# Key and query tiles woven into the last value tiles, in a gated attention and token-mixing kernel

## The chip, the cores and the metric

The kernel runs on one core of one Trainium2 chip. The metric is the device time of one launch in microseconds (us), the median of several runs. A profile of one execution shows five engines: PE (TensorE, with its weight loads as PEld), DVE (VectorE), ACT (ScalarE), POOL (GpSimd) and SP (SyncE), which here issues all DMAs.

## The reference

The result is a gated sum of two branches over the same x of 2048 rows and 512 columns:

```python
g = sigmoid((x * gate_w).sum(-1, keepdims=True))
a = softmax_attention(x @ wqkv, 32 heads of 16) @ wo
b = (W2 gelu(W1 layernorm(x)^T))^T          # mixes the 2048 tokens, F = 1792
out = g * a + (1 - g) * b
```

Everything is float32. Branch a takes q, k and v from one product with wqkv, and the softmax runs over all 2048 keys for each head. Branch b's layer norm needs mean and variance of each row.

## The kernel before, in words

Each float32 operand of a product is split into a high and a low part, and three products (high-high, high-low, low-high) are added in PSUM. One product tile of 128x512 over the 512 columns is therefore 12 matmuls.

The order of work is written out by hand: each engine runs its instructions in the order in which the program states them, and an instruction that waits holds up all behind it on that engine. This is true of SP as well, so a DMA that waits for data or for a free buffer holds up the later DMAs.

First stage, the tiles of v. x comes in 16 tiles of 128 rows. Tiles 0 to 3 are turned on PE. For the others x is loaded a second time in blocks of 32x128 (`load_blocks`, L198), turned by DVE (`turn_blocks`, L203), cast to the high part on ACT and reduced to the low part on POOL (`split`, L83 and L84). Each tile of x also has its row statistics and its gate sum made on DVE (`row_stats`, L211 to L214). PE forms v for tile t (`products`, L91), and ACT copies it out of PSUM (`v_out`, L237). In this stage PE has seven rotating banks of PSUM (`bank`). In the loop over t from 2 to 15 each pass states, in this order: turn blocks of tile t+2, row statistics of t-2, load blocks t+5, load x t+3, and the product for t. At t = 5 it also sets six stripes of the three key buffers to -1 on POOL (L321); these are the rows that multiply the shift of each query in the scores. v is stored to DRAM in three pieces (L234).

Second stage, key and query tiles. There are 32 tiles T of 128 columns by 512 tokens: four for the keys of 8 heads, four for their queries, and so on, four tiles for each set j = T // 4 of weight columns. Each set of columns is loaded (`load_wcols`, L150) and split; two sets are split in the first stage, the next ones by `bring_wcols` with two cuts on DVE (L915, L919). `tile_alone` runs one tile: 12 matmuls (L939), a copy to SBUF on ACT (L941, two buffers `qraw`), a cast to the high part (L596), the low part by subtraction on DVE (L599), the greatest magnitude on DVE (L587), for queries an absolute value times the keys' greatest (L603), and a store of the parts (L611, four buffers `pc`). Tiles T = 0 to 9 run so, one behind the other. Then the first keys (`load_k`) and queries (`load_q`), stored to DRAM, are read back in stacked form, 6 and 8 DMAs each (L646). `copy_v` copies the first two pairs of v on POOL.

Third stage, attention with products beside. The scores (L730) use 64 rows of the array; the other 64 work on one half of a key or query tile, or later of the second layer (L744). A phase has 12 units of scores, ACT and DVE empty them (L713, L720, L709: DVE parks some in SBUF, ACT takes exponentials), and the weighted sum with v follows (L780, 48 matmuls for a phase of 12 units). The seven banks of the phases are planned at build time by a search (`plan_banks`, `State`), which runs a small model of PE, ACT and DVE and picks a bank for each unit. A first short phase of 8 units has no product beside it. Tile T = 10 is run whole within the second phase, by a hook ahead of its seventh unit, and the planner's model has a term for it. Tiles 11 to 31 run as products beside the scores, one in each two phases; their later steps are jobs that run on DVE at the end of phases with room.

After the first 8 of 16 groups of attention come the layer norm and the first product of branch b, then the other 8 groups beside the second product and the output projection.

Of the kernel before, what the change touches and what calls it, by code (L numbers as in the profile page):

```python
# [76 lines left out]
def gated_mix(ctx: ExitStack, tc: tile.TileContext, a_x, a_wqkv, a_wo, b_w1, b_b1, b_w2, b_b2, gate_w, out):  # L77
# [78 lines left out]

    qk_cols = [c0 + b * P for b in range(ND) for c0 in (D, 0)]
    qk_w = []
    x_load = None

    with tc.tile_pool(name="vp", bufs=1, side="right") as pool:
# [8 lines left out]
        wv = []  # L170

        def load_wv(k):
            raw = pool.tile([P, D], F32, name=f"wv_raw{k}")
            nc.sync.dma_start(raw, a_wqkv.rearrange("(p k) c -> p k c", k=ND)[:, k, 2 * D : 3 * D])
            wv.append((raw, pool.tile([P, D], F32R, name=f"wv_hi{k}"), pool.tile([P, D], F32R, name=f"wv_lo{k}")))
# [63 lines left out]
        with tc.manual_schedule():  # L239
# [9 lines left out]
            warm(6)  # L249
            load(0)  # L250
# [53 lines left out]
            for t in range(2, NS):  # L304
                if t + 1 < TURNED:
                    turn(t + 1)
                if t + 2 < NS:
                    turn_blocks(t + 2)
                row_stats(t - 2)
                if t + 5 < NS:  # L310
                    load_blocks(t + 5)
                if t + 3 < NS:
                    load(t + 3)
                if t == 4:
                    turn_biases(bias_tiles)
                if t == 5:
                    pool.tile([P, 40], F32, name="pad")
                    for ks in k_bufs:
                        for i in range(2):
                            at = i * HALF + SHIFT[0]  # L320
                            nc.gpsimd.memset(ks[at : at + DH].bitcast(F32), -1.0)  # L321
                if t in (6, 9):
                    qk_w.append(load_wcols(qk_cols.pop(0)))
                if t in (9, 12):
                    qk_w.append(split_wcols(*qk_w.pop(0)))
                if t in (NS - 3, NS - 1):
                    store_v(*((0, 8) if t == NS - 3 else (8, 13)))
# [3 lines left out]
            for t in range(NS - 2, NS):  # L331
                row_stats(t)
            store_v(13, NS)
# [33 lines left out]
    ALONE_PE, ALONE_ACT = 2.75, 1.9  # L367
# [10 lines left out]
    class State:  # L378
# [8 lines left out]
        def clear(self):  # L387
            self.kept, self.banks, self.avail, self.homes, self.done, self.alone, self.next = {}, (), {}, {}, {}, (), 0
# [51 lines left out]
        def score(self, n, ops, parked, u, bank, since, alone):  # L440
# [4 lines left out]
            for _ in range(alone):  # L445
                at = min(range(RING), key=lambda b: new.free[b])
                new.pe = max(new.pe + TURN, new.free[at]) + ALONE_PE + TURN
                new.act = max(new.act, new.pe) + ALONE_ACT
                new.free[at] = new.act
                new.alone += ((u, at),)  # L450
# [13 lines left out]
        def place(self, n, ops, parked, u, alone):  # L464

            if u in self.kept:
                bank, since = self.kept[u]
                return self.score(n, ops, parked, u, bank, since, alone)
            op = next(op for op in ops if u in op)
            out = []  # L470
            for bank in range(RING):
                if self.free[bank] < NEVER:
                    if len(op) == 2 and u not in parked:
                        for other in (bank - 1, bank + 1):
                            if 0 <= other < RING and self.free[other] < NEVER:
# [3 lines left out]
                                out += new.score(n, ops, parked, u, bank, new.free[bank], alone)  # L479
                    else:  # L480
                        out += self.score(n, ops, parked, u, bank, self.free[bank], alone)
# [35 lines left out]
        def close(self, blocks):  # L517
# [8 lines left out]
            self.log = self.log, ("s", self.banks, homes, pairs, self.alone)  # L526
# [7 lines left out]
    def plan_banks(phases, free):  # L534
# [3 lines left out]
        for n, blocks, sets_now, beside, alone in phases:  # L538
            ops, parked = PLANS[n]
            for u in range(n):  # L540
                found = {}
                for new in sorted((new for old in best for new in old.place(n, ops, parked, u, alone.get(u, 0))), key=State.worth):
# [19 lines left out]
    kmax, qmax = {}, {}  # L562

    def qk_tile(T):

        j, n = divmod(T, NQ)
        b, is_q = divmod(j, 2)
        return j, b, is_q, n

    def qk_pairs(T):  # L570
        j, b, is_q, n = qk_tile(T)
        cols = slice(n * NB, (n + 1) * NB)
        hi, lo = qk_w[j]
        for k in range(ND):
            w, x = (hi[:, k, :], lo[:, k, :]), (xt_hi[:, k, cols], xt_lo[:, k, cols])
            yield from ((w[0], x[0]), (w[0], x[1]), (w[1], x[0]))

    def qk_parts(T, raw, pc, alone):

        j, b, is_q, n = qk_tile(T)  # L580
        low, high = (2, 0) if is_q else (1, 0)
        if n == 0:
            (qmax if is_q else kmax)[b] = small.tile([P, NQ], F32, name="qmax" if is_q else "kmax")
        most_of = (qmax if is_q else kmax)[b]

        def greatest():
            nc.vector.tensor_reduce(most_of[:, n : n + 1], raw, axis=AX.X, op=ALU.max, apply_absolute_value=True)  # L587
            if n == NQ - 1:
                nc.vector.tensor_reduce(most_of[:, 0:1], most_of, axis=AX.X, op=ALU.max)
                if is_q:  # L590
                    nc.vector.tensor_mul(most[:, b : b + 1], most_of[:, 0:1], kmax[b][:, 0:1])
                else:
# [334 lines left out]
    with tc.manual_schedule(engines=engines):  # L927
# [20 lines left out]
        for T in range(BEFORE):  # L948
# [19 lines left out]
            if T == NQ + 1:  # L968
                load_q(0)
# [551 lines left out]
```

## Time and profile before

| what | value |
|---|---|
| median of 3 runs | 1269.43 us (1267.03 to 1271.43) |
| the profiled execution | 1270.11 us, of which the profile's span is 1267.3 us |
| mean granted TensorE clock | 0.991 |
| busy: PE, ACT, DVE, POOL | 1243.3, 1080.7, 776.9, 213.9 us |
| last copy of v out of PSUM | begins at 56.75 us |
| last matmul of tile T = 9 | begins at 83.52 us |
| first exponential of the scores | begins at 93.02 us |

Times in the profile count from the start of the span. A row of a timeline gives start, duration, engine, line, operation, result and operands, and in brackets how long the engine was idle before it and what released it. PE's durations overlap from one matmul to the next, so steps are read from start to start.

### The profile page before, as it was taken

To read this page: it belongs to the slowest core of one execution; us is meant where nothing else is said; L and a number is where in the kernel's file an instruction comes from. 1 tells how busy PE (TensorE), PEld (TensorE's weight loads), DVE (VectorE), ACT (ScalarE), POOL (GpSimd) and SP (SyncE) were. 2 spreads that over 40 slices of the span, in tenths; PEclk is the share of its full clock that TensorE was granted. 3 is DMA by queue.
4 is the path that set the end of the run, shared out by engine and by line. 5 is a ranking of instruction groups with operands and counts; after the bars stand their busy time and mean duration, and the time that the engine had idled before them with its cause. 6 is when DMAs were issued, how large, how long until landed. Compare 5 with 4: busy or idle time off the path is not lost.

```text
span 1267.3 us, 33265 instructions
## 1 busy us (share of the span) xinstructions
PE 1243.3 (98%) x13446; PEld 799.5 (63%) x13446; DVE 776.9 (61%) x1317; ACT 1080.7 (85%) x1562; POOL 213.9 (17%) x345
## 2 busy tenths in 40 slices
PE   9979999999999999999999999999999999999998
PEld 6755565666678887566655666566655666565656
DVE  6746887878885347455554555545545656557974
ACT  4358999999834336999999999999999999999990
POOL 4500000000045445011111111111111111100000
PEclk9989999999999999899999999999999999999999
DMA  6664443553364433143224433433433443526742
GB/s 200 242 205 135 118 125 109 136 144 90 132 214 131 128 105 102 28 110 98 75 69 119 98 83 76 103 73 94 105 83 92 112 128 89 108 70 175 173 143 87
DMA packets 169919, 149.17 MB, mean 118 GB/s; under 512 B 82055, under 2 KB 127261, under 8 KB 169502
## 3 DMA queue, kind: packets, MB, share of 16 engines
q1 hardware_dynamic: 169758, 146.97, 42.6%
q8 instruction: 108, 1.77, 0.6%
q14 instruction: 53, 0.43, 0.1%
HBM read 108.50 MB, written 38.39 MB: 116 GB/s over the span
## 4 chain that ended last, share of the span: by engine, by line
PE 93%; DMA 2%; DVE 2%; ACT 1%; SPq 1%; POOL 1%; issue 0%; ACTq 0%; DVEq 0%; POOLq 0%
PE s L780 36%; PE s L730 35%; PE s L1178 12%; PE dn L744 5%; PE s L939 2%; PE acc L91 2%; PE pa L1397 2%; DMA row<-bp 1%; ACT pt L713 1%; DMA gw<-in_gate_w_dram 1%; DMA qp<-pc 0%; POOL ks L321 0%; DVE quad L720 0%; SPq L198 0%; PE dn L1397 0%
## 5 line engine op out<-in xcount | busy, mean ns | idle before, releaser
L713 ACT ACTIVATE pt<-s 128x512 f32<-128x512 f32 (+1 forms) x1217 | 717.0, 701 | 4.2 <-PE s L730 1.7
L730 PE MATMUL s<-qs,ks 64*128 64x512 f32 x2048 | 527.8, 405 | 13.1 <-DMA qs<-qp 6.2
L730 PEld LDWEIGHTS s<-qs,ks 64*128 64x128 f32 x2048 | 353.8, 185 | 174.1 <-ACT pt L713 74.5
L720 DVE COPY quad<-s 128x512 f32<-128x512 f32 x616 | 400.8, 687 | 59.4 <-PE dn L744 33.5
L780 PE MATMUL s<-pt,vt 128*17 128x256 f32 x5728 | 423.3, 381 | 1.3 <-DVE quad L720 1.3
L709 ACT ACTIVATE quad<-quad 128x2048 f32<-128x2048 f32 x154 | 300.1, 1949 | 1.6 <-DVE quad L720 1.6
L780 PEld LDWEIGHTS s<-pt,vt 128*17 128x17 f32 x5728 | 181.5, 97 | 166.4 <-ACT pt L713 53.0
L792 DVE TENSOR_TENSOR ot<-s,ot 128x256 f32<-128x256 f32 (+1 forms) x155 | 79.4, 512 | 306.3 <-PE s L780 215.7
L744 PE MATMUL dn<-u,w_hi 64*128 64x512 f32 x768 | 255.9, 406 | 0.0
L780 PE MATMUL s<-quad,vt 128*17 128x256 f32 x2464 | 226.8, 379 | 0.0
L1009 POOL TENSOR_TENSOR w_lo<-w_raw,w_hi 128x512 fp32r<-128x512 f32 (+1 forms) x127 | 149.6, 1184 | 101.8 <-ACT w_hi L1006 78.4
L749 POOL MEMSET token<- 1x1 f32 x154 | 17.9, 116 | 870.5 <-PE dn L744 771.6
L744 PE MATMUL dn<-u,w_lo 64*128 64x512 f32 x384 | 155.9, 406 | 0.0
L780 PEld LDWEIGHTS s<-quad,vt 128*17 128x17 f32 x2464 | 100.9, 98 | 60.7 <-issue 0.8
L744 PEld LDWEIGHTS dn<-u,w_hi 64*128 64x128 f32 x768 | 136.3, 185 | 1.6 <-POOL token L749 0.2
L1178 PE MATMUL s<-h,w_hi 128*128 128x512 f32 x392 | 121.1, 390 | 0.0
L1006 ACT CAST w_hi<-w_raw 128x512 fp32r<-128x512 f32 (+1 forms) x64 | 36.1, 566 | 58.4 <-PE s L1178 30.0
L1178 PEld LDWEIGHTS s<-h,w_hi 128*128 128x128 f32 x392 | 73.5, 188 | 15.7 <-ACT w_hi L1006 0.4
L1178 PE MATMUL s<-h,w_lo 128*128 128x512 f32 x196 | 76.9, 392 | 0.0
L744 PEld LDWEIGHTS dn<-u,w_lo 64*128 64x128 f32 x384 | 70.9, 185 | 1.0
L744 PE MATMUL dn<-xt_hi,wc_hi 64*128 64x512 f32 x168 | 70.7, 421 | 0.0
L744 PE MATMUL dn<-xt_lo,wc_hi 64*128 64x512 f32 x168 | 66.3, 395 | 0.0
(190 smaller groups left out, 1176.0 us busy)
## 6 DMA issues: line engine op xcount, KB each, us to landing
ks<-kp SPq DMA_DIRECT2D x384, 64.0 KB
w_raw<-in_B_w_dram SPq DMA_DIRECT2D x96, 256.0 KB
qs<-qp SPq DMA_DIRECT2D x256, 64.0 KB
qp<-pc SPq DMA_DIRECT2D x16, 768.0 KB
x<-in_A_x_dram SPq DMA_DIRECT2D x32, 256.0 KB
kp<-pc SPq DMA_DIRECT2D x16, 512.0 KB
vt<-v_d SPq DMA_DIRECT2D x30, 272.0 KB
w_raw<-in_B_w_dram SPq DMA_DIRECT2D x32, 128.0 KB
```

The costliest lines, as they stand in the source:

```text
L91: nc.tensor.matmul(ps, a, b, start=start and n == 0, stop=stop and n == last)
L709: act = nc.scalar.activation(dst, dst, AF.Exp, scale=SCALE)
L713: act = nc.scalar.activation(dst, banks[:, at[0] : at[-1] + 1, :], AF.Exp, scale=SCALE)
L720: reads(nc.vector.tensor_copy(homes[op][:, op.index(u), :], banks[:, units[u][5], :]), units[u][5])
L730: mm = nc.tensor.matmul(banks[:, bank, :], kt[2 * grp + c * P // SH][rows, c * P % SH : c * P % SH + P], qt[grp][rows, qb * NB : (qb + 1) ...
L744: mm = nc.tensor.matmul(ps, a[half], b[half], start=first and not second, stop=last and bool(second))
L780: mm = nc.tensor.matmul(av[32 * j : 32 * j + VC, at : at + QC], vt[grp][:, c, i, :], pt[:, h * QC : (h + 1) * QC], start=m == 0, stop=m == ...
L792: reads(nc.vector.tensor_tensor(x, added, x, ALU.add), bank)
L939: writes(nc.tensor.matmul(banks[:, bank, :], a, b, start=n == 0, stop=n == 3 * ND - 1), bank)
L1006: copy(hi, raw)
L1009: sub(lo, raw, hi.bitcast(F32), ALU.subtract)
L1178: mm = nc.tensor.matmul(banks[:, bank, :], a, h[c][:, b, :], start=c == 0 and k == 0, stop=c == NS - 1 and k == 2)
```

## The change

Six tiles, T = 0 to 5 (the four key tiles of the first set and two query tiles), move into the first stage: tiles 0, 1 and 2 stand between v tiles 11 and 12, and tiles 3, 4 and 5 between v tiles 12 and 13. They use the first stage's banks, two `qraw` buffers and two `pc` buffers, which are the same memory as the raw v weights. Of each woven tile the copy and the cast are stated at once, and the subtraction, the greatest magnitude, the absolute value and the store one pass later. Tiles 6 to 10 run alone after the last tile of v. The hook in the second phase and the planner's term for it go.

The six memsets of -1 are stated ahead of the first load instead of at t = 5. In each pass the load of x is stated ahead of the load of blocks, where it was behind it. Row statistics of tiles 10 to 15 are stated later, beside the woven tiles. The pieces of v that are stored are tiles 0 to 7, 8 to 11 and 12 to 15 instead of 0 to 7, 8 to 12 and 13 to 15. Key loads 0 to 2 and query loads 0 and 1 are stated within and at the end of the first stage. The square root of the row statistics is stated ahead of the exponential of the gate, both after tile 6. Tile 10's high part is cast on DVE instead of ACT. The columns for j = 2 are split in the first stage, for j = 3 ahead of tile 8, and for j = 4 in jobs of the later phases.

```diff
+        taken = [pool.tile([P, 3, NB], F32R, name="pc", bufs=2) for _ in range(2)]
+        wv_raw = [tile[:, n, :].bitcast(F32) for tile, n in ((taken[0], 0), (taken[0], 1), (taken[0], 2), (taken[1], 0))]
...
             warm(6)
+            for ks in k_bufs:
+                for i in range(2):
+                    at = i * HALF + SHIFT[0]
+                    nc.gpsimd.memset(ks[at : at + DH].bitcast(F32), -1.0)
             load(0)
...
-            for t in range(2, NS):
-                if t + 1 < TURNED:
-                    turn(t + 1)
-                if t + 2 < NS:
-                    turn_blocks(t + 2)
-                row_stats(t - 2)
-                if t + 5 < NS:
-                    load_blocks(t + 5)
-                if t + 3 < NS:
-                    load(t + 3)
...
+            def woven(T):
+
+                ps = bank()
+                for n, (a, b) in enumerate(qk_pairs(T)):
+                    nc.tensor.matmul(ps, a, b, start=n == 0, stop=n == 3 * ND - 1)
+                raw = pool.tile([P, NB], F32, name="qraw", bufs=2)
+                nc.scalar.copy(raw, ps)
+                steps, store = qk_parts(T, raw, parts_of(pool, T, bufs=2), True)
+                steps[0][1]()
+
+                def rest():
+                    for n in (2, 1, 3):
+                        if n < len(steps):
+                            steps[n][1]()
+                    store()
+
+                last.append(rest)
...
+            order = [*range(2, 12), "0", "1", "2", 12, "3", "4", "5", 13, 14, 15]
+            calls = {
+                4: [lambda: qk_w.update({0: load_wcols(qk_cols.pop(0))})],
+                7: [lambda: qk_w.update({0: split_wcols(*qk_w[0])}), lambda: qk_w.update({1: load_wcols(qk_cols.pop(0))})],
+                10: [lambda: qk_w.update({1: split_wcols(*qk_w[1])}), lambda: store_v(0, 8)],
+                13: [lambda: store_v(8, 12)],
+                14: [lambda: cuts.update({18: bring_wcols(2)})],
+                17: [lambda: load_k(0)],
+                18: [lambda: load_k(1)],
+                19: [lambda: load_k(2), lambda: load_q(0)],
+            }
+            cuts = {}
+            stats = {**{i: [i] for i in range(10)}, 13: [10], 14: [11], 15: [12], 16: [13], 17: [14], 18: [15]}
+            for i, what in enumerate(order):
+                if i == 0:
+                    turn(TURNED - 1)
+                if TURNED + i < NS:
+                    turn_blocks(TURNED + i)
+                if i == 2:
+                    turn_biases(bias_tiles)
+                for t in stats.get(i, ()):
+                    row_stats(t)
+                    if t + 5 < NS:
+                        load(t + 5)
+                if i + 7 < NS:
+                    load_blocks(i + 7)
+                if i == 3:
+                    pool.tile([P, 40], F32, name="pad")
+                while last:
+                    last.pop(0)()
+                for call in calls.get(i, ()):
+                    call()
+                for cut in cuts.get(i, ()):
+                    cut()
+                if isinstance(what, str):
+                    woven(int(what))
+                else:
+                    v_tile(what)
+            assert not last
+            store_v(12, NS)
+            load_q(1)
...
-            steps, store = qk_parts(T, raw, parts_of(qe, T, bufs=4), True)
+            steps, store = qk_parts(T, raw, parts_of(qe, T, bufs=4), T < ALONE - 1)
...
-        for T in range(BEFORE):
+        for T in range(WOVEN, ALONE):
             turn_of.rotate(-1)
+            if T == WOVEN:
+                cuts[T + 2] = bring_wcols(3)
+            if T == WOVEN + 3:
+                jobs.extend((two + 1, *step) for step in zip((0.45, 0.7), bring_wcols(4)))
+            for cut in cuts.pop(T, ()):
+                cut()
             tile_alone(T, turn_of[0])
-            if T == 0:
+            if T == WOVEN:
+                nc.vector.tensor_scalar_add(w_, mv[:, :, 1], EPS)
+                nc.scalar.activation(y, w_, AF.Sqrt)
                 nc.scalar.activation(e, z, AF.Exp, scale=-1.0)
...
-            if T in (1, 2):
-                copy_v(T - 1)
-            if T in (1, NQ - 1, NQ + 2):
-                load_k((1, NQ - 1, NQ + 2).index(T))
-            if T == NQ + 1:
-                load_q(0)
-        load_q(1)
+            if T < WOVEN + 2:
+                copy_v(T - WOVEN)
...
-        alone = {6 + 4 * m: 1 for m in range(ALONE - BEFORE)}
...
-        planned, v_banks, free = plan_banks([mixed, *future(4, sizes, alone)], [{turn_of[-1]: 2.0, turn_of[0]: 3.0}.get(b, 0.0) for b in range(RING)])
-        hooks = {u: (lambda bank, T=BEFORE + m: tile_alone(T, bank)) for m, u in enumerate(alone)}
+        planned, v_banks, free = plan_banks([mixed, *future(4, sizes)], [{turn_of[-1]: 2.0, turn_of[0]: 3.0}.get(b, 0.0) for b in range(RING)])
```

More of the change, by code (lines that the diff above doesn't have):

```diff
@@ new lines, in copy_v, with qk_tile, qk_pairs @@
+    def copy_v(g):
+        pair = groups[g][1]
+        vt[g] = vt_pool.tile([P, NS, 2, VC], F32, name="vt")
+        nc.gpsimd.tensor_copy(vt[g], v[:, :, 2 * pair : 2 * pair + 2])
+    kmax, qmax = {}, {}
+    def qk_tile(T):
+        j, n = divmod(T, NQ)
+        b, is_q = divmod(j, 2)
+        return j, b, is_q, n
+    def qk_pairs(T):
+        j, b, is_q, n = qk_tile(T)
+        cols = slice(n * NB, (n + 1) * NB)
+        hi, lo = qk_w[j]
+        for k in range(ND):
+            w, x = (hi[:, k, :], lo[:, k, :]), (xt_hi[:, k, cols], xt_lo[:, k, cols])
+            yield from ((w[0], x[0]), (w[0], x[1]), (w[1], x[0]))
@@ L537, in plan_banks @@
         sets = 0
-        for n, blocks, sets_now, beside, alone in phases:
+        for n, blocks, sets_now, beside in phases:
             ops, parked = PLANS[n]
@@ L808, in future @@
                     BESIDE[n][second],
-                    dict(alone) if pos == 4 and not second else {},
                 )
```

229 lines of the change are left out of this document (90 added, 139 removed).

## The prediction

> **What bounds the kernel now.** I read the page's totals first, then the windows of the first 120 us, then the timelines of each engine around the two stretches that stand out.
>
> ```profile
> span 1267.3 us, 33265 instructions
> ...
> PE 1243.3 (98%) x13446; PEld 799.5 (63%) x13446; DVE 776.9 (61%) x1317; ACT 1080.7 (85%) x1562; POOL 213.9 (17%) x345
> ```
>
> TensorE is busy for 98% of the span. What is idle is little, 24.0 us, so the question is where it lies and which of it the change touches. Windows of 10 us (columns: length, PE, PEld, DVE, ACT, POOL busy with counts, granted clock, DMA share, GB/s):
>
> ```profile
> 30.00:40.00 10.00, 7.26 (x25) 5.53 (x25) 6.31 (x12) 2.83 (x5) 7.58 (x7) 0.83 0.66 186
> ...
> 80.00:90.00 10.00, 4.67 (x19) 3.19 (x17) 6.23 (x12) 2.74 (x5) 0.00 (x0) 0.90 0.66 209
> 90.00:100.00 10.00, 7.40 (x26) 4.95 (x27) 1.38 (x2) 6.76 (x9) 0.00 (x0) 0.59 0.93 285
> 100.00:110.00 10.00, 7.98 (x74) 4.63 (x73) 6.17 (x10) 7.72 (x11) 0.09 (x1) 1.00 0.54 161
> 110.00:120.00 10.00, 10.00 (x134) 5.95 (x134) 7.12 (x14) 9.88 (x13) 0.18 (x2) 1.00 0.26 77
> ```
>
> Most of the idle time lies here: 2.74 us among the tiles of v (30:40) and 9.95 us where the scores begin (80:110), with the granted clock down to 0.83 and 0.59. From 110 us on TensorE and ScalarE are both full, and the chain shows a fixed rhythm; the first and the nineteenth block of weighted v:
>
> ```profile
> 110.48 2.72 PE s L780 x48
> ...
> 213.29 2.71 PE s L780 x48
> ```
>
> (213.29 - 110.48)/18 = 5.71 us a phase. The change leaves the phases' work as it is, so a stage that begins earlier should end earlier by as much. Two terms are to be priced: the stall at 31 us and the junction from 84 to 107 us.
>
> **Term 1: the minus ones go first.** Timelines of POOL, PE and ACT:
>
> ```profile
> 24.51 1.80 POOL L84 TENSOR_TENSOR xt_lo<-xw,xt_hi 128x512 fp32r<-128x512 f32 x1 [0.75 <-ACT xt_hi L83]
> 26.37 5.88 POOL L321 MEMSET ks<- 16x1024 f32 x6
> ...
> 33.64 0.80 PE L91 MATMUL acc<-wv_hi,xt_lo 128*128 128x512 f32 x1 [2.74 <-POOL xt_lo L84]
> ```
>
> ```profile
> 27.77 0.59 ACT L237 COPY v<-acc 128x512 f32<-128x512 f32 x1 [0.93 <-PE acc L91]
> ...
> 30.49 0.59 ACT L237 COPY v<-acc 128x512 f32<-128x512 f32 x1 [1.26 <-PE acc L91]
> ...
> 37.71 0.59 ACT L237 COPY v<-acc 128x512 f32<-128x512 f32 x1 [2.32 <-PE acc L91]
> ```
>
> Six memsets hold POOL for 5.88 us and the xt_lo pieces queue behind them. The copies of v follow at 30.49 - 27.77 = 2.72 us a tile, and at 37.71 - 30.49 = 7.22 us over the stall: it costs 4.50 us, idle time and the matmuls at half clock behind it together. Set first, the memsets run from about 1.4 to 7.3 us, where POOL has only the two bias memsets (their DMAs) and the ones of v to wait:
>
> ```profile
> 1.13 0.29 POOL masks.py:199 TENSOR_SCALAR_AFFINE_SELECT ident<-ident 128x128 f32<-128x128 f32 x1
> ...
> 3.52 0.88 PEld L182 LDWEIGHTS acc<-ident,x 128*128 128x128 f32 x4 [0.48 <-issue]
> ...
> 8.44 1.00 SPq L220 DMA_DIRECT2D bias<-in_B_b_dram  x2
> ```
>
> The bias tiles would be clear at about 7.8 us, still before SP comes to them at 8.44. If all six got ahead of the identity's second half at 1.13, the first transposes (3.52) would start near 7.3: 3.8 us lost. I take nothing, since the identity is written first in the program, and keep 0 to 3.8.
>
> **The other order of early loads** puts x(i+5), which waits for the row statistics of tile i, ahead of the four block loads, so block t is issued where block t+1 is now, one turn of about 2.4 us later:
>
> ```profile
> 18.28 1.86 SPq L198 DMA_DIRECT2D xb<-in_A_x_dram  x4
> ...
> 20.67 2.89 SPq L198 DMA_DIRECT2D xb<-in_A_x_dram  x4
> ```
>
> ```profile
> 22.68 1.09 DVE L203 STREAM_TRANSPOSE xw<-xb 128x512 f32<-128x512 f32 x1
> ...
> 25.07 1.11 DVE L203 STREAM_TRANSPOSE xw<-xb 128x512 f32<-128x512 f32 x1
> ```
>
> Block 7 would be issued by 20.14 and turned at 22.68, block 8 by 23.56 and turned at 25.07. Landing is not shown for these; the nearest row is the queries' (below: issued by 88.68, used at 90.89), 2.2 us. Block 8 is then 0.7 us late. From the turn to the end of xt_lo lie 24.51 + 1.80 - 22.68 = 3.63 us, so its xt_lo is there at 29.4, and PE wants it at 30.5. Nothing, with 1.1 us of cover; without it up to 2 us. Range 0 to 2. Sum of term 1: 4.5.
>
> **Term 2: six tiles among those of v, five behind them.** The product work of TensorE stays the same; only its order moves. The last tile of v ended with its copy at 56.75 in the old order:
>
> ```profile
> 56.75 0.59 ACT L237 COPY v<-dn 128x512 f32<-128x512 f32 x1 [2.13 <-PE dn L91]
> ```
>
> With term 1 and six tiles of 2.72 it ends at 56.75 - 4.5 + 16.3 = 68.6, the sixth woven tile (T5) at 68.6 - 3 x 2.72 = 60.4, the eleventh tile (T10) at 68.6 + 13.6 = 82.2. Now the junction as it is, in PE's timeline:
>
> ```profile
> 83.52 0.39 PE L939 MATMUL s<-xt_hi,wc_lo 128*128 128x512 f32 x1
> 89.23 0.76 PE L730 MATMUL s<-qs,ks 64*128 64x512 f32 x1 [5.32 <-DMA qs<-qp]
> 90.89 1.19 PE L730 MATMUL s<-qs,ks 64*128 64x512 f32 x3 [0.89 <-DMA qs<-qp]
> ...
> 98.33 0.49 PE L939 MATMUL s<-xt_hi,wc_hi 128*128 128x512 f32 x1
> ...
> 102.04 0.50 PE L730 MATMUL s<-qs,ks 64*128 64x512 f32 x1 [0.68 <-ACT qraw L941]
> ...
> 105.30 1.92 PE L780 MATMUL s<-pt,vt 128*17 128x256 f32 x32 [1.34 <-DVE quad L720]
> 107.15 0.50 PE L730 MATMUL s<-qs,ks 64*128 64x512 f32 x1
> ```
>
> The steady phases begin at 107.15. What holds them is ScalarE's start on the exponentials, and ahead of it the queues:
>
> ```profile
> 83.23 0.43 DVE L915 CAST wc_hi<-wc_raw 128x512 fp32r<-128x512 f32 x1 [7.61 <-DMA wc_raw<-in_A_wqkv_dram]
> ```
>
> ```profile
> 76.94 0.72 ACT L603 ACTIVATE pc<-qraw,kmax 128x512 fp32r<-128x512 f32 x1
> ...
> 85.75 0.59 ACT L941 COPY qraw<-s 128x512 f32<-128x512 f32 x1 [5.37 <-DVE qmax L587]
> 86.36 0.62 ACT L596 CAST pc<-qraw 128x512 fp32r<-128x512 f32 x1
> ...
> 91.72 1.28 ACT L713 ACT_TABLE_LOAD   x1 [3.54 <-PE s L730]
> 93.02 4.88 ACT L713 ACTIVATE pt<-s 128x512 f32<-128x512 f32 x7
> ```
>
> ```profile
> 78.53 0.55 SPq L150 DMA_DIRECT2D wc_raw<-in_A_wqkv_dram  x1
> 79.18 1.28 SPq L611 DMA_DIRECT2D qp<-pc  x1
> 85.10 3.58 SPq L646 DMA_DIRECT2D qs<-qp  x8
> ...
> 97.43 5.40 SPq L646 DMA_DIRECT2D qs<-qp  x8
> ```
>
> Keys and queries: today the query store (through 80.46) lands before 85.10, the first queries land at 89.23. In the new order T5's store goes out after its copy, cast and Abs (0.59 + 0.62 + 0.72) near 62.7, with room for the 4.6 us of that landing: the key loads stand ahead of the query loads, which go out at about 71 to 74.7. They land well before 82.2: this wait goes.
>
> What is late next are the weight columns for tile 12 on, on SP. From 62.7 SP issues T5's store, 18 key loads, 16 query loads and one store of v, then wc_raw, and only then the stores of T6 on. At 3.58/8 = 0.45 us each these 36 take 16.2 us: wc_raw goes at 78.9. At the crowded row (5.40/8 = 0.675) it would be 24.3 us and 87.0; since none of the 34 loads waits for data by then, I take 0.45. Landing took 83.23 - 78.53 = 4.7 us behind two query stores, and 2.2 for queries alone; with a store of v and queries ahead I take 4.0, so DVE cuts at 82.9. DVE stands at that cut with T8's subtraction and maximum behind it, which hold one of two raw buffers that T10's copy on ACT needs; from cut to that copy 85.75 - 83.23 = 2.52 us, and 0.6 for the copy itself. The exponentials begin at 82.9 + 2.5 + 0.6 = 86.0 instead of 93.02. T10's cast goes to DVE and is no longer between. Behind T10's copy wait all exponentials on ACT, and TensorE, once six banks are full.
>
> From there to the steady phases it takes 107.15 - 93.02 = 14.1 us today. In it lie T10 and its wait (102.04 - 98.33 = 3.7), which leave, and the 1.34 us of DVE, blocked by T10's parts and a cut, which leaves too: 9.1. The half-clock stretch is in it (0.59 in that window); with a shorter idle ahead some of it should go. The floor is ACT's 4.88 us, a block of 1.92 and the last scores between, some 7.5. I take the middle, 8.3. Steady phases then begin at 94.3, a gain of 107.15 - 94.3 = 12.9 for both terms. The early end, T10's copy with no wait for DVE: 82.2 + 0.6 + 7.5 = 90.3, a gain of 16.9. The late end: wc_raw at 87.0, cut at 91.7, exponentials at 94.8, phases at 94.8 + 9.1 = 103.9, a gain of 3.3.
>
> ScalarE's two table loads stay two (Sqrt, then Exp), but both lie now behind T6; the 1.28 us at 91.72 go from the exponentials' start, and are in the 7.0 us just found. Behind T6 they delay T7's copy by about 2.2 us, which the slack of 2.72 - 1.93 us a tile takes back by T10. The Trainium skill ("ScalarE: Activation LUTs", What ACT_TABLE_LOAD costs) gives about 2.66 us for each switch of tables, its drain included; two of them behind T6 would be 5.3 us, an estimate from that page, where the row of 1.28 makes 2.6, and T10's copy would come at about 85.5, still no later than the wait for DVE lets it.
>
> The cut of the columns for tile 16 on becomes two jobs of DVE in later phases, 1.1 us where DVE is busy 7.12 of 10: nothing. The woven tiles have two buffers for their pieces, so each cast on ACT waits for the store two tiles back: 4.6 us of landing against 5.44 between the tiles, less 1.9 for copy, cast and subtraction, so about 1 us late. Behind it on ACT stand the copies of v; TensorE turns through seven banks and doesn't wait for them: nothing, and if the banks ran out, 1 us for each of four tiles. The stores of v keep three pieces; the first two go out ahead of the tiles' and key stores.
>
> **The sum.** 1270.1 us (its own time, span 1267.3 and 2.8 around it) - 12.9 = 1257.2, of which 4.5 are term 1 and 8.4 the junction. The median of three was 1269.4, 0.7 below; I take 1257.
>
> **The clock.** The stall of 2.74 us was answered with 0.83 in its window, as the 7.22 us show. The new gap, from six filled banks at 83.6 to the first freed one near 86.6, is as long: a half-clock stretch as in 30:40 cost 4.50 - 2.74 = 1.8 us, and the 8.3 above holds it. The Trainium skill ("TensorE: Matmul & The Clock Gate", HAM oscillation) lets idle gaps up to about 3.4 us pass without a slower clock; by it the new gap would be free and the time some 1.8 us lower. The trace doesn't agree with that bound, since 2.74 us was enough.
>
> **Rivals.** (a) *The junction is queue-bound*: SP issues at 0.675, gain 3.3 to 9, about 1264. For it: 97.43; against: 85.10. (b) *ACT starts at once*: columns land early, gain 15 to 17, about 1254. For it: the queue's traffic is lighter; against: 7.61 us of wait at 83.23. (c) *Only the memsets count*: the end of T10 to the steady phases keeps its length, 23.3 - 2.7 = 20.6 us, because loads wait for stores as now; gain 4.5 less what a late identity or a late block takes (1 to 2): about 1267. Against: queries are stored 20 us ahead. (d) *The phases get longer*: banks of all 42 phases are planned anew from another start, without T10. One bank freed one exponential later (93.02: 4.88/7 = 0.70 us) in each of the 41 phases after the first costs 28.6: 1257 + 28.6 = 1286. It decides from 12.9/41 = 0.31 us a phase. Against: 5.71 held for eighteen phases, the plan's sizes are the same.
>
> **How the numbers follow.** Forecast (gain 9.5 to 15) 0.60; (a) 0.14; (b) 0.12; (c) 0.08; (d) 0.06. A measurement of this kernel tells 0.3%, 3.8 us. Faster: 0.60 + 0.14 + 0.12 = 0.86; same 0.08; slower 0.06. The range leaves out (c), (d) and the ends of the others: 1252 to 1264.5.
>
> **What would show it.** Right: no idle of TensorE at 31 us and clock 1.00 in 30:40; T10's last product near 82; queries landed before it; first exponential at 85 to 88 with no table load ahead; steady phases from 93 to 96 at 5.71. Wrong: TensorE waiting for xt_lo or xb among the v tiles; SP reaching the columns after 83; phases longer than 5.8 us.

## The result, and the profile after

The changed kernel takes 1259.12 us (median of four, 1258.5 to 1261.29) against 1269.19 us beside it: a ratio of 0.9924, interval 0.9903 to 0.9945. The forecast was 1257 in a range of 1252 to 1264.5. The profiled execution, 1261.29 us, is the longest of the four. Its totals and its windows of 10 us (columns as in the prediction):

```profile
span 1258.4 us, 33255 instructions
...
PE 1242.6 (99%) x13446; PEld 800.6 (64%) x13446; DVE 776.1 (62%) x1318; ACT 1079.2 (86%) x1561; POOL 215.7 (17%) x345
```

```profile
30.00:40.00 10.00, 10.00 (x46) 8.29 (x45) 7.70 (x18) 4.75 (x9) 7.00 (x5) 1.00 0.76 218
...
80.00:90.00 10.00, 6.63 (x26) 4.42 (x26) 3.46 (x7) 5.42 (x8) 0.00 (x0) 0.78 0.93 267
90.00:100.00 10.00, 8.32 (x55) 4.21 (x54) 4.77 (x8) 5.75 (x8) 0.09 (x1) 0.53 0.83 285
100.00:110.00 10.00, 9.94 (x127) 5.98 (x129) 7.48 (x14) 9.63 (x14) 0.18 (x2) 1.00 0.16 48
```

TensorE's idle time at 31 us is gone and the clock there is 1.00. At the junction idle time is left, and the clock there, 0.53, is lower than before (0.59). The chain of waits, first and twenty-first block of weighted v:

```profile
102.65 2.72 PE s L829 x48
...
216.88 2.71 PE s L829 x48
```

(216.88 - 102.65)/20 = 5.71 us a phase, as before. PE's timeline at the junction:

```profile
81.62 0.39 PE L963 MATMUL s<-xt_hi,wc_lo 128*128 128x512 f32 x1
...
83.16 0.70 PE L779 MATMUL s<-qs,ks 64*128 64x512 f32 x3 [0.73 <-DMA qs<-qp]
86.38 2.20 PE L779 MATMUL s<-qs,ks 64*128 64x512 f32 x5 [2.52 <-ACT pt L764]
...
93.25 0.79 PE L779 MATMUL s<-qs,ks 64*128 64x512 f32 x1 [1.68 <-DVE quad L771]
...
95.68 3.62 PE L829 MATMUL s<-pt,vt 128*17 128x256 f32 x32
99.22 0.54 PE L779 MATMUL s<-qs,ks 64*128 64x512 f32 x1
```

The product tiles end where the forecast had them, at 82, but the steady phases begin at 99.22: 7.93 us before the 107.15 of the old kernel, where 12.9 were forecast. TensorE waits first for ACT's exponentials, then for a park on DVE. Their timelines:

```profile
54.69 0.62 ACT L226 CAST pc<-qraw 128x512 fp32r<-128x512 f32 x1 [4.70 <-DMA kp<-pc]
...
68.44 0.59 ACT L347 COPY v<-dn 128x512 f32<-128x512 f32 x1 [1.91 <-PE dn L91]
...
82.39 0.58 ACT L965 COPY qraw<-s 128x512 f32<-128x512 f32 x1 [1.82 <-DVE kmax L217]
85.73 4.89 ACT L764 ACTIVATE pt<-s 128x512 f32<-128x512 f32 x7 [2.76 <-DMA v_d<-v]
```

```profile
37.81 1.08 DVE L313 STREAM_TRANSPOSE xw<-xb 128x512 f32<-128x512 f32 x1 [2.16 <-DMA xb<-in_A_x_dram]
...
45.55 1.11 DVE L313 STREAM_TRANSPOSE xw<-xb 128x512 f32<-128x512 f32 x1 [1.88 <-DMA xb<-in_A_x_dram]
...
79.95 0.42 DVE L256 CAST wc_hi<-wc_raw 128x512 fp32r<-128x512 f32 x1
...
90.84 0.43 DVE L226 CAST pc<-qraw 128x512 fp32r<-128x512 f32 x1 [7.35 <-DMA qp<-pc]
...
92.51 1.88 DVE L771 COPY quad<-s 128x512 f32<-128x512 f32 x3
```

Each of the two engines stands behind a DMA. The exponentials (85.73) wait 2.76 us for the last store of v: their result tiles lie in memory that v held until then, so it must have been read out. T10's cast (90.84), which the change put on DVE, waits 7.35 us for the store of a query tile, T6: the later pool has four piece buffers for the tiles T6 to T10, so T10 takes the one of T6. Behind that cast stand the parks of the scores. Why both stores are late is on SP's queue:

```profile
63.56 0.55 SPq L150 DMA_DIRECT2D wc_raw<-in_A_wqkv_dram  x1
65.75 0.38 SPq L241 DMA_DIRECT2D qp<-pc  x1
66.18 9.83 SPq L170 DMA_DIRECT2D ks<-kp  x18
76.05 4.89 SPq L170 DMA_DIRECT2D qs<-qp  x8
81.03 0.38 SPq L344 DMA_DIRECT2D v_d<-v  x1
81.45 4.87 SPq L170 DMA_DIRECT2D qs<-qp  x8
86.43 0.93 SPq L241 DMA_DIRECT2D qp<-pc  x2
```

From 66.18 SP issues 18 key loads (9.83/18 = 0.55 us each) and 16 query loads (0.61 each). The store of v, ready with its copy at 69.0, goes out at 81.03; T6's and T7's go out at 86.43 in one row. T6's parts are complete when DVE's subtraction ends, at 73.30, so its store lost 13 us in the queue.

### The profile page after: what moved, and what is told of

Its sections match the earlier page's. It is cut to its first block, busy times and chain, and to the rows that moved or that the text cites. A ratio compares the mean times of both kernels' runs of the same rounds, so it can differ in the third digit from the quotient of the medians.

```text
span 1258.4 us, 33255 instructions
## 1 busy us (share of the span) xinstructions
PE 1242.6 (99%) x13446; PEld 800.6 (64%) x13446; DVE 776.1 (62%) x1318; ACT 1079.2 (86%) x1561; POOL 215.7 (17%) x345
## 4 chain that ended last, share of the span: by engine, by line
PE 90%; DMA 3%; DVE 2%; SPq 2%; ACT 1%; issue 1%; DVEq 0%; ACTq 0%
PE s L829 36%; PE s L779 36%; PE s L1201 12%; PE dn L793 4%; PE pa L1420 2%; SPq L170 1%; DMA kp<-pc 1%; DMA row<-bp 1%; DMA xb<-in_A_x_dram 1%; ACT pt L764 1%; DVE xw L313 1%; SPq L308 1%; PE acc L388 1%; DMA v_d<-v 0%; DMA qp<-pc 0%
```

## The experiments

All times stand against the kernel before, run beside them (1269.5 us for the first four, 1268.89 for the next four, 1269.54 for the last three). "Steady" is the first score behind the first block of 32 matmuls, as 99.22 above.

| kernel | us (range) | ratio (interval) | first exponential | T10's cast | steady | span |
|---|---|---|---|---|---|---|
| before (profile) | 1269.19 | 1 | 93.02 | | 107.15 | 1267.3 |
| changed (profile) | 1259.12 (1258.5 to 1261.29) | 0.9924 (0.9903 to 0.9945) | 85.73 | 90.84 | 99.22 | 1258.4 |
| changed, again | 1259.98 (1258.67 to 1260.61) | 0.9927 (0.9914 to 0.9941) | 84.88 | 90.00 | 97.20 | 1257.1 |
| third key piece, second queries behind T10 | 1254.41 (1252.54 to 1255.33) | 0.9885 (0.987 to 0.99) | 82.53 | 83.70 | 91.20 | 1250.8 |
| last store of v first | 1258.48 (1258.14 to 1258.74) | 0.9917 (0.9904 to 0.9931) | 84.73 | 89.64 | 95.26 | 1255.4 |
| fifth piece buffer | 1256.22 (1255.47 to 1257.31) | 0.9897 (0.9882 to 0.9912) | 85.51 | 83.32 | 95.01 | 1254.4 |
| before + memsets first | 1264.94 (1263.91 to 1266.6) | 0.9972 (0.996 to 0.9983) | 88.05 | | 101.89 | 1261.9 |
| before + T10 behind T9 | 1272.8 (1271.0 to 1274.74) | 1.0029 (1.0017 to 1.0042) | 95.78 | | 109.66 | 1271.0 |
| changed, blocks ahead of x | 1257.68 (1257.12 to 1258.35) | 0.991 (0.9895 to 0.9925) | 83.77 | 88.87 | 95.84 | 1255.4 |
| changed, Exp ahead of Sqrt | 1259.25 (1258.58 to 1259.91) | 0.9925 (0.991 to 0.9941) | 85.38 | 89.39 | 95.00 | 1255.8 |
| late group, again | 1252.98 (1251.73 to 1254.74) | 0.9869 (0.9852 to 0.9887) | 83.34 | 84.60 | 90.99 | 1251.9 |
| late group, blocks ahead of x | 1254.45 (1253.59 to 1256.24) | 0.9882 (0.9865 to 0.9898) | 82.60 | 83.14 | 90.25 | 1253.9 |
| the same, fifth buffer | 1254.95 (1254.37 to 1255.88) | 0.9889 (0.9873 to 0.9906) | 82.62 | 83.16 | 91.53 | 1252.4 |

Span less steady is 1159.2 to 1161.3 us in all but one row (1163.7, see the last part of this section). So what a kernel gains is settled, to within some 2 us, by the time at which its steady phases begin. Differences smaller than that are read from the medians.

**The queue of loads behind T5.** Is SP's row of loads what holds both engines?

```diff
-                19: [lambda: load_k(2), lambda: load_q(0)],
+                19: [lambda: load_q(0)],
...
             store_v(12, NS)
-            load_q(1)
...
             if T < WOVEN + 2:
                 copy_v(T - WOVEN)
+        load_k(2)
+        load_q(1)
```

> The changed kernel, but key load 2 and query load 1 (group 1) are stated behind tile 10 instead of ahead of tile 6, so SP issues the last store of v and the stores of tiles 6 and 7 fourteen DMAs sooner. Theory Q (the junction is held by what stands on SP ahead of the last store of v and of tile 6's store): v's store goes at about 77.5 us instead of 81.0 and lands near 82; the first exponential at about 83.0 instead of 85.7 (now held by tile 10's copy); tile 6's store lands by 83, so DVE does not wait for its piece buffer (7.35 us before); steady phases from about 92 instead of 99.2; time 1252. Rival C (the start of the phases costs 13.5 us from the first exponential whatever stands on SP, by half clock and ACT's filling): steady phases at 83.0 + 13.5 = 96.5, time 1256.5.

It takes 1254.41 us, 5.6 less than the changed kernel run beside it. Timelines of ACT, DVE, PE and SP in this kernel:

```profile
82.05 0.58 ACT L964 COPY qraw<-s 128x512 f32<-128x512 f32 x1 [1.82 <-DVE kmax L217]
82.53 4.90 ACT L763 ACTIVATE pt<-s 128x512 f32<-128x512 f32 x7
```

```profile
83.70 0.43 DVE L226 CAST pc<-qraw 128x512 fp32r<-128x512 f32 x1 [0.54 <-ACT pt L763]
```

```profile
89.35 1.92 PE L828 MATMUL s<-pt,vt 128*17 128x256 f32 x32
91.20 0.49 PE L778 MATMUL s<-qs,ks 64*128 64x512 f32 x1
```

```profile
77.39 0.37 SPq L344 DMA_DIRECT2D v_d<-v  x1
77.86 1.50 SPq L241 DMA_DIRECT2D qp<-pc  x2
```

The store of v goes out 3.6 us earlier than in the first profile and the stores of the tiles 8.6 us earlier; the exponentials follow T10's copy at once, and DVE no longer waits for a store. From the first exponential to the steady phases it is now 8.7 us, close to the 8.3 of the prediction. The steady phases, at 91.20, decide for theory Q (92) against the rival (96.5); the time fell between the two, 2.4 us above the 1252 of theory Q. The queue is the cause; which of the two stores counts is for the next two.

**The store of v alone.** The last store of v ahead of the first query loads instead of between the two query groups:

```diff
-                19: [lambda: load_k(2), lambda: load_q(0)],
+                19: [lambda: load_k(2)],
...
             store_v(12, NS)
+            load_q(0)
             load_q(1)
```

> The changed kernel, but the last store of v is stated ahead of query load 0 instead of behind it; all else stays, so tile 6's store still goes at about 86.4 us. It takes away one of two waits. Theory Q1 (DVE's wait for tile 6's store sets the steady phases): the first exponential comes at about 83.3 instead of 85.7, DVE still waits for tile 6's store until about 90.8, steady phases stay at 99: time 1259. Rival Q2 (the start of the exponentials sets them): steady phases 2.4 us sooner, time 1256.7.

1258.48 us, 1.5 less than the changed kernel beside it. ACT and DVE:

```profile
84.73 4.81 ACT L765 ACTIVATE pt<-s 128x512 f32<-128x512 f32 x7 [1.27 <-PE s L780]
```

```profile
89.64 0.43 DVE L226 CAST pc<-qraw 128x512 fp32r<-128x512 f32 x1 [5.67 <-DMA qp<-pc]
```

ACT's wait for the store has gone, so that store was what held it. But the exponentials start at most 1.0 us sooner (85.73 and 84.88 in the two profiles of the changed kernel), because the queries are now behind the store and the scores come later. DVE's wait for T6's store stays. The time is what theory Q1 said, but the difference of 1.5 us is not clear of the scatter: the two ranges and the intervals of the ratios overlap. The steady phases came at 95.26, sooner than either theory had them. That can't be put down to the store, since this profile also has only 3.4 us of half clock, where the changed kernel's two have 13.8 and 10.4 (last section).

**The piece buffer alone.**

```diff
-            steps, store = qk_parts(T, raw, parts_of(qe, T, bufs=4), False)
+            steps, store = qk_parts(T, raw, parts_of(qe, T, bufs=5), False)
...
-            steps, store = qk_parts(T, raw, parts_of(qe, T, bufs=4), T < ALONE - 1)
+            steps, store = qk_parts(T, raw, parts_of(qe, T, bufs=5), T < ALONE - 1)
```

> The changed kernel with five piece buffers instead of four for the tiles run alone and beside the scores, so tile 10's cast on DVE waits for no store. It takes away the other wait. Theory Q1 (DVE's wait for tile 6's store sets the steady phases): the first exponential stays at 85.7, DVE is through with tile 10 by 86, steady phases at 85.7 + 8.3 to 9.1 = 94 to 95, time 1254.5. Rival Q2 (the exponentials' start, held by v's store, sets them): steady phases stay at 99, time 1259.

1256.22 us, 3.8 less than the changed kernel beside it, and below its range. ACT, then DVE:

```profile
85.51 4.88 ACT L764 ACTIVATE pt<-s 128x512 f32<-128x512 f32 x7 [2.63 <-DMA v_d<-v]
```

```profile
83.32 0.42 DVE L226 CAST pc<-qraw 128x512 fp32r<-128x512 f32 x1
```

The exponentials are as late as before, but T10's cast runs 7 us earlier and the parks are no longer behind it. The steady phases come at 95.01, as theory Q1 had them, and the rival's 99 and 1259 fall. So the wait for the piece buffer costs about 3.8 us by the medians, and these two ranges do not overlap. With the 1.5 of the store of v, which is not firm, it comes near the 5.6 of the late group. The profiles of the two single edits do not show the split: both have their steady phases at 95.0 to 95.3, the one with the fifth buffer with 6.8 us of half clock, the other with 3.4.

**How much two executions of the same kernel differ.** The changed kernel again:

> The changed kernel once more, as the reference for the three others on the same chip: 1259 by every theory. The profiled execution had a mean granted clock of 0.991 and was the slowest of four, the others 0.993 to 0.995 and 2 to 3 us shorter; if the length of the half-clock stretch at the junction is chance (theory W), its length here differs from 13.65 us by a whole number of 3.4 us and the time with it by about 1.7 us each; if it is set by the waits alone, it is 13.65 again.

```profile
80.00:90.00 10.00, 7.11 (x31) 5.07 (x30) 3.55 (x7) 6.10 (x10) 0.00 (x0) 0.78 0.98 286
90.00:100.00 10.00, 8.31 (x67) 4.38 (x64) 6.76 (x11) 6.97 (x10) 0.09 (x1) 0.70 0.74 251
```

1259.98 us. The cast of T10 is at 90.00, 0.84 sooner than in the first profile, the steady phases 2.02 sooner. The other 1.2 us go with the clock: 0.53 in the first profile's window and 0.70 here, with the same instructions. In windows of 1 us the half clock runs from 85.7 to 99.3 in the first profile and from 85.7 to 95.9 here, one piece of 3.4 us less, which is the step that theory W named. That this is chance is not shown: the idle time that ends with DVE's park ends at 93.25 in the first profile and at 92.41 here, and the longer stretch may come from that. From T10's cast to the steady phases it is 8.38 and 7.20 us in these two, and 5.6 in the two kernels where the cast waits as well but the clock is 0.97 or 1.00 in the window of 90:100 (last store of v first, Exp ahead of Sqrt).

**The memsets alone**, in the kernel before: the six memsets stated behind `warm(6)` instead of at t = 5, and nothing else.

```diff
             warm(6)
+            for ks in k_bufs:
+                for i in range(2):
+                    at = i * HALF + SHIFT[0]
+                    nc.gpsimd.memset(ks[at : at + DH].bitcast(F32), -1.0)
...
                     pool.tile([P, 40], F32, name="pad")
-                    for ks in k_bufs:
-                        for i in range(2):
-                            at = i * HALF + SHIFT[0]
-                            nc.gpsimd.memset(ks[at : at + DH].bitcast(F32), -1.0)
```

> The kernel before with one edit: the six memsets of -1 stated ahead of the first load. Theory (the stall at 31 us costs 4.50 us and nothing after it fills the room): TensorE has no idle time at 31 us, the last copy of v begins at 52.2 instead of 56.75, the steady phases 4.5 us sooner, time 1269.5 - 4.5 = 1265.0. Rival (the junction waits for transfers with their own dates and gives part back): the last copy of v at 52.2, but the steady phases less than 3 us sooner, time above 1266.5.

1264.94 us, 3.95 less than before (interval of the ratio 0.996 to 0.9983, so 2.2 to 5.1 us). The last copy of v begins at 52.13, where 52.2 was expected; the first exponential comes at 88.05, 4.97 sooner, and the steady phases at 101.89, 5.26 sooner. The term of 4.5 holds, also without the rest of the change.

**T10 ahead alone**, in the kernel before:

```diff
-    ALONE, BEFORE = 11, 10
+    ALONE, BEFORE = 11, 11
```

T10 then runs right behind T9 instead of within the second phase.

> The kernel before with one edit: tile 10 runs alone behind tile 9 instead of within the second phase, nothing is woven into the v tiles. TensorE's wait of 5.32 us for queries at 83.9 would be filled with tile 10's 2.72 us. Theory (what holds the phases is their data and DVE, tile 10 fits into the wait): the first exponential stays at about 93, the steady phases begin 3.7 us sooner, without tile 10 and its wait, time 1265.8. Rival (tile 10's copy, cast and parts stand ahead of the exponentials on ACT and DVE, and its columns are the ones that come late): the exponentials start up to 3 us later, time 1268 to 1270.

1272.8 us: slower, by 3.9 us, more than either expectation. ACT and SP:

```profile
93.85 0.62 ACT L596 CAST pc<-qraw 128x512 fp32r<-128x512 f32 x1 [5.22 <-DMA qp<-pc]
94.49 1.28 ACT L713 ACT_TABLE_LOAD   x1
```

```profile
86.11 3.58 SPq L646 DMA_DIRECT2D qs<-qp  x8
89.80 0.40 SPq L611 DMA_DIRECT2D qp<-pc  x1
```

What it met is the piece buffer. T10's cast, here on ACT, needs the buffer of T6, whose store goes out behind the query loads at 89.80. ACT stands 5.22 us, the exponentials begin at 95.78, and with them the rest. The half clock is longer too, 20.4 us at the junction against 10.2 in the kernel before (reckoned from windows as in the last section), so how much of the 3.9 us is the wait alone stays open. In the changed kernel T10's cast stands on DVE; that takes this wait off ACT, and the same wait is then DVE's.

**The order of early loads alone**, undone in the changed kernel:

```diff
                 for t in stats.get(i, ()):
                     row_stats(t)
-                    if t + 5 < NS:
-                        load(t + 5)
                 if i + 7 < NS:
                     load_blocks(i + 7)
+                for t in stats.get(i, ()):
+                    if t + 5 < NS:
+                        load(t + 5)
```

> The changed kernel with the old order of early loads: blocks ahead of x in each pass. In the changed kernel DVE waits twice, 4.0 us in all, for blocks. Theory (those waits are covered, TensorE has no idle time before 82 us): DVE's waits go, nothing else moves, time 1260 as the reference run. Rival (the order matters through SP, since the loads end sooner and the stores of v and keys with them): the queries' loads and v's last store come earlier, steady phases 1 to 2 us sooner, time 1258.

```profile
73.85 5.04 SPq L170 DMA_DIRECT2D qs<-qp  x8
78.99 0.37 SPq L344 DMA_DIRECT2D v_d<-v  x1
```

1257.68 us, against 1259.98 and 1259.12 for the changed kernel in its own two comparisons and 1259.25 for the next kernel, run beside this one; the ranges of all three lie above its own. The intervals of the ratios overlap (0.9895 to 0.9925 and 0.9914 to 0.9941), so the size, 1.4 to 2.3 us, is not firm. The time is the rival's. The trace shows what moved: with the blocks ahead, the query loads go out at 73.85, against 76.05 and 75.11 in the changed kernel's two profiles and 74.45 in the next kernel's; the store of v goes out at 78.99 against 81.03, 80.13 and 79.35, and T10's cast comes at 88.87. The sizes scatter, but the direction holds in every profile: T5's store goes out at 63.2 to 64.0 us in the three kernels with the old order and at 64.4 to 65.8 in the seven with the new. TensorE does not wait among the tiles of v in either order. So the new order costs, as far as the traces show, through a queue 30 us later.

**The order of the tables**, Exp ahead of Sqrt in the changed kernel, so that a load of Exp's table falls before the first exponential:

```diff
             if T == WOVEN:
-                nc.vector.tensor_scalar_add(w_, mv[:, :, 1], EPS)
-                nc.scalar.activation(y, w_, AF.Sqrt)
                 nc.scalar.activation(e, z, AF.Exp, scale=-1.0)
...
+                nc.vector.tensor_scalar_add(w_, mv[:, :, 1], EPS)
+                nc.scalar.activation(y, w_, AF.Sqrt)
```

> The changed kernel with the exponential of the gate ahead of the square root, as in the kernel before, so a table load of 1.28 us stands ahead of the first exponential of the scores. Theory H (the load waits behind the same wait as the exponential): the load begins when v's store has landed, near 85, exponentials at 86.5, phases about 1.3 us later, time 1261.3. Rival (the load runs while ACT waits for v's store): the load at about 83, exponentials at 85 to 85.7, time 1260.

```profile
84.09 1.28 ACT L764 ACT_TABLE_LOAD   x1 [1.94 <-DMA v_d<-v]
85.38 4.88 ACT L764 ACTIVATE pt<-s 128x512 f32<-128x512 f32 x7
```

1259.25 us: no difference that can be told. Theory H is right about the load: it does not use the wait, it stands behind it, and the exponentials begin 1.28 us later for it. The 1261.3 of theory H did not come, since DVE's cast at 89.39 comes last.

**A version that beats both, and what is left in it.** The kernel with the late group, once more and with two additions: the blocks ahead of x, and that with a fifth buffer too.

> The same kernel as in the run with the third key piece and the second query group behind tile 10, as the measure for the two kernels beside it: 1254.4 us as there, within 1 us.

> Third key piece and second query group behind tile 10, and the four block loads ahead of x(i+5) as in the old order. Theory (the order of the early loads counts only through SP's queue: it moves the last store of v and T6's store by 2 us): with the second group late, T10's copy and the first exponential no longer wait for the queue (82.05 and 82.53), so nothing is left to gain: within 0.8 us of the kernel with the group late alone, first exponential at 82.0 to 82.6. Rival (the order counts by itself, through the blocks that DVE waited for, 4.0 us at 37.8 and 45.5): 1.5 to 2.3 us faster than that kernel, 1252.4.

> The same and a fifth piece buffer in the later pool. Theory (the wait for a piece buffer is the one that the late group already takes away): no difference to the kernel beside it, within 0.8 us, steady phases at 91 to 91.5. Rival (the fifth buffer helps by itself, since later tiles also wait for stores): 1 to 3 us faster.

1252.98, 1254.45 and 1254.95 us. Neither addition makes it faster, so both rivals fall: with the loads out of the way the order of early loads and the piece buffer have next to nothing left to give (in the late group's second profile T10's cast, at 84.60, still waits 0.63 us for a store). That agrees with their acting through the waits for the two stores. The second is 1.5 us slower than the first rather than within 0.8; the intervals overlap (0.9852 to 0.9887 and 0.9865 to 0.9898). Its profile lost its lead far from the junction. It was 0.56 us ahead at the last weighted v of the first eight groups (331.55 against 332.11) and 1.47 behind at the second of the next eight (506.09 against 504.62). On the way TensorE waits for the layer norm (0.57 us of idle time at 351.69, none in the late group), and the first weighted v of the second eight groups takes 4.69 us instead of 3.74, in a stretch of half clock that lasts longer. Why these differ was not followed further. The late group is thus the version to keep: 1254.41 and 1252.98 us in two runs, 1.2 and 1.3% below before, and 5.6 us below the change where the two ran side by side.

## Why the prediction was right, and where not

- **Term 1, the memsets: right.** T10's last matmul came at 81.62; one tile behind T9's 83.52, less 4.5, it should come at 83.52 + 2.72 - 4.5 = 81.74. The copy of the last v tile was forecast for 68.6 and came at 68.44. Alone the edit gave 3.95 us.
- **The other order of early loads at nothing: mis-sized, 1.4 to 2.3 us.** The blocks were late (DVE waited 2.16 and 1.88 us for them; with the old order put back, 1.30 us once), more than the 0.7 forecast, and TensorE did not wait, as the prediction had it. But the step priced only TensorE's cover. SP's later entries moved as well, T5's store by 0.3 to 2.5 us over ten profiles.
- **The woven tiles' casts at 1 us late: mis-sized.** The first waited 4.70 us for its piece buffer. TensorE's banks hid it, as forecast, but T5's store went out at 65.75 instead of 62.7 (the prediction's own terms, 60.4 + 0.59 + 0.62 + 0.72, make 62.3), and all loads behind it with it.
- **The queries' wait goes: nearly right.** 5.32 us became 0.73.
- **"What is late next are the weight columns": wrong.** The step took the queue's order from the program text, where the columns follow all loads. SP issued them at 63.56, ahead of the loads, and DVE cut them at 79.95 without a wait. So SP does not keep the order of the program text throughout, contrary to what the description of the kernel before says of it. The queue itself was as the step described it, and longer: 34 loads and a store of v take 20.1 us (66.18 to 86.32), 0.58 each, between the two prices of the prediction, 0.45 and 0.675. What it made late were the stores behind it. The step priced no wait for the memory that is taken over from v, and none for the four piece buffers of the tiles run alone.
- **The exponentials at 86.0: right in time, for another reason.** They came at 85.73, held by the last store of v. The 1.82 us that T10's copy waited for DVE did exist, but were not last. That the number agrees is luck.
- **8.3 us from there to the steady phases: wrong, 13.5.** This is the step that lost the gain. The prediction took DVE's stay away ("blocked by T10's parts and a cut, which leaves too"), while the change moves T10's cast to DVE, ahead of the parks and behind T6's store. Without that wait the stretch is 9.5 (fifth buffer) and 8.7 us (late group). The half clock added to it: 8.38 us from the cast on, where 5.6 were enough at full clock.
- **The sum.** Junction forecast 8.4, measured 7.93 - 4.5 = 3.4 in the first profile and 9.95 - 4.5 = 5.5 in the second. The median came out 2 us above the forecast. Part of that is luck: the range was wide enough for most of rival (a) too, and the steady phases, at 99.22 and 97.20, lie outside the 93 to 96 that the prediction named as a sign of being right. Its other signs came true: no idle time at 31 us, T10 at 82, the first exponential at 85 to 88 without a table load, phases of 5.71; only the queries did not quite land before T10's end.
- **Rivals.** Phases did not get longer (5.71). (a), the junction bound by the queue, is nearest to what happened in mechanism, though it too had the columns as the last to arrive. Its gain of 3.3 to 9 holds the 7.93 us of the first profile's steady phases, but not the 9.95 of the second, nor the 10.1 between the medians, which lies in the forecast's own 9.5 to 15. (b) asked for ACT to start at once; it is what the late group does, 1254.41 and 1252.98 beside a forecast of 1254.
- **The clock.** Half speed came again, at 85.7, within the gap of 2.52 us that ends at 86.38, as at 33.4 within the 2.74 of the old kernel. The Trainium skill ("TensorE: Matmul & The Clock Gate", HAM oscillation) lets gaps up to about 3.4 us pass; the trace again does not agree. With the last store of v first, gaps of 0.50, 0.70, 0.50 and 0.42 us between 82.5 and 86.8 were enough for half speed from 87.2.

## What to carry to other kernels

When work is moved ahead, list what each engine's next instruction waits for, taken-over memory and rotating buffers among them, and look where the store that frees it stands in its queue: here loads that nothing needed yet stood ahead of two stores that two engines were waiting for. Putting those loads behind the stores gave 5.6 us, more than half of what the whole change had brought. An edit that costs nothing where it is made can still push a queue that is used up 30 us later, so take the order of a queue from the trace and not from the program text.

## What the runs showed of the hardware

**Half clock comes in pieces of one length.** In windows of 1 us the clock of the junction shows 1.00 or 0.50, and other values only where it changes. So the time at half is twice the shortfall of a window. The kernel with T10 ahead has the longest stretch:

```profile
80.00:90.00 10.00, 6.50 (x29) 5.06 (x27) 6.23 (x12) 3.19 (x6) 0.00 (x0) 0.94 0.56 177
90.00:100.00 10.00, 5.07 (x18) 3.05 (x20) 0.00 (x0) 6.12 (x8) 0.00 (x0) 0.50 0.99 302
100.00:110.00 10.00, 7.29 (x54) 3.49 (x52) 5.02 (x9) 5.60 (x7) 0.09 (x1) 0.54 0.52 161
```

Here it is 1.2 + 10 + 9.2 = 20.4 us. In the first profile of the changed kernel it is 4.4 + 9.4 = 13.8, in the second 4.4 + 6.0 = 10.4, with the late group one window at 0.83, 3.4, and none in its second run. These are about six, four, three and one times 3.4 us. The same kernel can thus lose one piece more or less, and its two profiles differ by 1.2 us from T10's cast to the steady phases. The changes also keep a beat. In the kernel before and in the one with T10 ahead the clock falls twice, in these windows:

```profile
33.00:34.00 1.00, 0.36 (x1) 0.36 (x2) 0.38 (x1) 0.00 (x0) 1.00 (x2) 0.71 0.89 220
88.00:89.00 1.00, 0.00 (x0) 0.00 (x0) 1.00 (x3) 0.18 (x1) 0.00 (x0) 0.51 0.51 164
```

```profile
34.00:35.00 1.00, 1.00 (x4) 0.78 (x3) 1.00 (x2) 0.52 (x1) 0.56 (x1) 0.57 0.64 159
88.00:89.00 1.00, 0.00 (x0) 0.00 (x0) 1.00 (x2) 0.59 (x1) 0.00 (x0) 0.88 0.49 148
```

By their shortfalls it falls at 33.42 and 88.02 in the first, at 34.14 and 88.76 in the second: 54.6 us apart in both, sixteen times 3.41, and 0.7 us later in the second, although TensorE's wait at 31 us ends there at 33.36 instead of 33.64. The Trainium skill ("TensorE: Matmul & The Clock Gate", Part 1: The HAM clock gate) describes a window of about 3.4 us that runs freely, so that its phase differs from run to run; these rows agree.

**A table load stands behind its activation's wait**: 84.09, behind the store of v. No drain is seen beside its 1.28 us; the exponential follows at 85.38. In the changed kernel an activation ends at 73.15, a table load runs from 73.17, and the next activation begins at 74.47.

**Small loads in a row fill the issuing queue**: 34 loads in 19.6 us (9.83 + 4.89 + 4.87), 0.58 us each, and what stood behind them waited although it was ready: the last store of v 12 us, T6's store 13 us.
